# A fused sliding-window attention and MLP kernel: sums apart from products in the opening, four hidden tiles over four banks, stores on another queue

## The chip, the cores and the metric

The kernel runs on one core of a Trainium2 chip. A core has five engines that run side by side, each with its own queue of instructions in order: TensorE (PE in the profile, with its weight loads as PEld), VectorE (DVE), ScalarE (ACT), GpSimd (POOL) and SyncE (SP, which here only issues DMAs). They work on SBUF, TensorE writes its results to PSUM (eight banks), and DMAs move data between the outer memory and SBUF. The metric is the time of one execution on the device, in microseconds (us).

## The reference

Eight batches, eight heads, 576 tokens, head size 64, all inputs in float32. Attention is limited to a window of 32 tokens on either side; its output, with the heads side by side, goes through an MLP of 512 to 2048 to 512 with a leaky ReLU.

```python
scores = scale * np.matmul(q, k.transpose(0, 1, 3, 2))        # scale = 1/8
mask = np.abs(pos[:, None] - pos[None, :]) <= 32
scores = np.where(mask, scores, -1e9)
attn = np.exp(scores - np.max(scores, axis=-1, keepdims=True))
attn = attn / (np.sum(attn, axis=-1, keepdims=True) + 1e-09)
x = np.matmul(attn, v).transpose(0, 2, 1, 3).reshape(4608, 512)
h = x @ w_in                                                   # 512 x 2048
out = np.maximum(0.01 * h, h) @ w_out                          # 2048 x 512
```

## The kernel before

The attention of one batch is cut into eight steps, numbered through all batches: step `i` belongs to batch `i // 8`, half `(i // 4) % 2` of the tokens (288 each) and head pair `i % 4`. Two heads are handled as one: their keys and values stand on the diagonal of 128 x 128 blocks (`kbd`, `vbd`), the rest of which is zero and is cleared once.

What one step does:

- `score(i)`, lines 237 to 253: five matmuls into the PSUM tile `ps` (one buffer of two banks), the exponential `e` on ScalarE, and the product with the window's mask, `pr`, on GpSimd.
- `weighted(i)`, lines 268 to 294: the sums of the probabilities `s` (matmul with a block of ones) and the weighted values `x` (five matmuls with `vbd`), one PSUM bank each; then on VectorE the reciprocal `r` of the sums and the product of `x` and `r`, which lands in `xT`. From step 12 on, `join` first adds the two parts of `pr` on VectorE, so that the sums need one matmul in place of two.

Ahead of them stand, for each pair, the cast of `q` and `k` to bf16 (`cast_qk`), their transposes (on TensorE for batches 0 to 2, with ScalarE copying them out as `qT` and `kT`; by DMA from batch 3 on), `place_keys` (two copies on VectorE into `kbd`), and the cast of the values into `vbd` (`cast_v`, on GpSimd, or in the opening on ScalarE).

The MLP works on halves of 288 tokens: `h_tile(g, f)` (lines 300 to 311) takes four matmuls, one for each head pair, for one of 16 blocks of the hidden width, and an activation on ScalarE into `gT`. `o_tile(j)` (lines 313 to 328) takes 16 matmuls for 128 tokens, a copy `o_sb` on ScalarE and a store that ScalarE issues itself. `h` tiles, output tiles and TensorE's transposes share four PSUM banks (`mmps`).

The order of the work is the order of the program; nothing is rescheduled. The opening (lines 420 to 488) is written out by hand. It loads batch 0 on SP (lines 89 to 96), runs steps 0 to 3 with two or three matmuls without use between them (`keep_busy`), issues the weights' DMAs from GpSimd in between, then loads the keys of batch 1, runs the 16 `h` tiles of half 0 with steps 4 to 7 among them, and the 16 of half 1 with the transposes of batch 1 and scores 8 and 9. The loads of batch 1 are held back by a tiny DMA that reads a weight: the `q` and `k` loads behind the second part of `w_in` (line 459), the `v` loads behind the second part of `w_out` (line 473).

From line 493 on a plan of quarter output tiles and `h` tiles with estimated durations decides when the next step is due; `spend` runs the due steps before each item. In a step of batches 1 to 6 the casts, DMA transposes and loads of later batches are issued too, the DMAs all from SP.

Of the kernel before, what the change touches and what calls it, by code (L numbers as in the profile page):

```python
# [16 lines left out]
def kernel(  # L17
# [31 lines left out]
    cast = ctx.enter_context(tc.tile_pool(name="cast", bufs=1))  # L49
    attn = ctx.enter_context(tc.tile_pool(name="attn", bufs=2))  # L50
    kt = ctx.enter_context(tc.tile_pool(name="kt", bufs=4))
    prob = ctx.enter_context(tc.tile_pool(name="prob", bufs=4))
    tdma = ctx.enter_context(tc.tile_pool(name="tdma", bufs=1))
    outp = ctx.enter_context(tc.tile_pool(name="outp", bufs=4))
    PS = bass.MemoryType.PSUM
# [62 lines left out]
    def clear(t, p):  # L118
        flat = t[:, p].rearrange("p n j -> p (n j)")
        nc.scalar.activation(  # L120
            out=flat, in_=zero.to_broadcast([128, NB * 128]), func=AF.Copy,
        )

    nc.vector.memset(kbd[0], 0.0)
    clear(vbd[0], 0)
    clear(vbd[0], 1)

# [8 lines left out]
    for lo in (0, 64):  # L138
        w = win[lo:lo + 64]
        nc.gpsimd.affine_select(  # L140
            out=w, in_=w, compare_op=ALU.is_ge, fill=0.0,
            base=0, channel_multiplier=-1, pattern=[[0, 3], [1, 128]],
        )
        nc.gpsimd.affine_select(
            out=w, in_=w, compare_op=ALU.is_ge, fill=0.0,
            base=2 * W, channel_multiplier=1, pattern=[[0, 3], [-1, 128]],
        )
    win_f = win.rearrange("p n c -> p (n c)")
    mask = [const.tile([128, NCOL], BF16, name=f"mask{i}") for i in range(2)]

# [86 lines left out]
    def score(i):  # L237
        b, hf, p = where(i)
        ps = scps.tile([128, 1024], FP32, name="ps")
        c0 = 512 - HALF  # L240
        for blk, q0, n in WIN[hf]:
            nc.tensor.matmul(  # L242
                ps[:, c0:c0 + n], kbd[b % 2][:, p, blk],
                qT[b][:, p, q0:q0 + n], start=True, stop=True,
            )
            c0 += n
        e = attn.tile([128, NCOL], BF16, name="e")
        nc.scalar.activation(  # L248
            out=e, in_=ps[:, 512 - HALF:512 - HALF + NCOL], func=AF.Exp, scale=scale,
        )  # L250
        pr = prob.tile([128, NCOL], BF16, name="pr")
        nc.gpsimd.tensor_mul(pr, e, mask[hf])  # L252
        probs[i] = pr, None

    def join(i):


        hf = where(i)[1]
        pr = probs[i][0]
        both = prob.tile([128, HALF], BF16, name="both")  # L260
        o0 = ODD[hf]
        o1 = o0 + NCOL - HALF
        nc.vector.tensor_add(both[:, o0:o1], pr[:, o0:o1], pr[:, HALF:NCOL])  # L263
        rest = slice(0, o0) if o0 else slice(o1, HALF)
        nc.vector.tensor_copy(out=both[:, rest], in_=pr[:, rest])  # L265
        probs[i] = pr, both

    def weighted(i):
        b, hf, p = where(i)
        pr, both = probs.pop(i)  # L270
        x = xps.tile([128, HALF], FP32, name="x")
        s = xps.tile([128, HALF], FP32, name="s")
        if both is not None:
            nc.tensor.matmul(s, ones_bd, both, start=True, stop=True)  # L274
        else:
            nc.tensor.matmul(
                s, ones_bd, pr[:, 0:HALF], start=True, stop=False, skip_group_check=True,
            )
            nc.tensor.matmul(
                s[:, ODD[hf]:ODD[hf] + NCOL - HALF], ones_bd, pr[:, HALF:NCOL],  # L280
                start=False, stop=True, skip_group_check=True,
            )
        c0 = 0
        for n_, (blk, q0, n) in enumerate(WIN[hf]):
            a = q0 - HALF * hf
            nc.tensor.matmul(  # L286
                x[:, a:a + n], vbd[b % 2][:, p, blk, :], pr[:, c0:c0 + n],
                start=(n_ == 0), stop=(n_ == len(WIN[hf]) - 1), skip_group_check=True,
            )
            c0 += n  # L290
        r = attn.tile([128, HALF], FP32, name="r")
        nc.vector.reciprocal(r, s)  # L292
        t0 = (b * S + hf * HALF) % RING
        nc.vector.tensor_mul(xT[:, p, t0:t0 + HALF], x, r)  # L294

    gT = const.tile([128, FFC, RING], BF16)

    def h_tile(g, f):  # L300

        t0 = g * HALF % RING
        h = mmps.tile([128, 512], FP32, name="mm", tag="mm")
        for c in range(DMC):
            nc.tensor.matmul(  # L305
                h[:, 0:HALF], w_in_bf[:, c, ts(f, 128)], xT[:, c, ds(t0, HALF)],
                start=(c == 0), stop=(c == DMC - 1),
            )
        nc.scalar.activation(  # L309
            out=gT[:, f, ds(t0, HALF)], in_=h[:, 0:HALF], func=AF.Prelu, alpha=0.01,  # L310
        )

    def o_tile(j, hook=None):


        cols = (0, 512) if j < NTOK // 128 - 1 else (0, 384, 512)
        for lo, hi in zip(cols[:-1], cols[1:]):
            o = mmps.tile([128, 512], FP32, name="mm", tag="mm")
            for f in range(FFC):
                if hook and lo == 0 and f % 4 == 0:  # L320
                    hook()
                nc.tensor.matmul(  # L322
                    o[:, lo:hi], gT[:, f, ds(128 * j % RING, 128)], w_out_bf[:, f, lo:hi],
                    start=(f == 0), stop=(f == FFC - 1),
                )
            o_sb = outp.tile([128, DMODEL], FP32, name="o_sb")
            nc.scalar.activation(out=o_sb[:, lo:hi], in_=o[:, lo:hi], func=AF.Copy)  # L327
            nc.scalar.dma_start(out=out[ts(j, 128), lo:hi], in_=o_sb[:, lo:hi])

    def keep_busy(n):  # L330


        t = mmps.tile([128, 512], FP32, name="mm", tag="mm")
        for _ in range(n):
            nc.tensor.matmul(t, ones_bd, mask[0][:, 0:512], start=True, stop=True)


    NC = 2 * NPAIR * B
# [22 lines left out]
    def step():  # L361
# [7 lines left out]
        if b > 0:  # L369
            upto = 8 * (b + 1) + (PLAN[b > 1][0][r] if b + 1 < BY_DMA else 0)  # L370
            step_transposes(max(upto - 1, 8 * (b + 1)))
        if i < 7:
            score(i + 1)
        elif 8 <= i < NC - 2:
            nb, _, np_ = where(i + 2)
            if nb >= BY_DMA:
                step_transposes(8 * nb + 2 * np_ + 2)
                place_keys()
            score(i + 2)
# [42 lines left out]
    def first_pair():  # L422
        next(first)
        next(first)
        place_keys()
# [3 lines left out]
    cast_qk(0, 1, nc.vector)  # L429
    first_pair()  # L430
    first_pair()
    clear(vbd[0], 2)
    cast_v(0, 0)
    cast_qk(0, 2, nc.vector)
    score(0)
    load_w_in(0, 512)
    first_pair()
    clear(vbd[0], 3)
    cast_qk(0, 3, nc.vector)
    load_w_in(512, 1024)  # L440
    for i in range(NPAIR):
        score(i + 1)
        if i + 1 < NPAIR:
            cast_v(0, i + 1, on_act=True)
        if i < 2:
            load_w_in(1024 + 512 * i, 1536 + 512 * i)
        else:
            load_w_out(i - 2)
        if i > 0:
            keep_busy(3 if i == 1 else 2)  # L450
        weighted(i)
        if i == 0:
            first_pair()
    state["done"] = NPAIR

    for p in range(NPAIR):
        load_qk(1, p, w_in_bf[0:1, 0, 512:514] if p == 0 else None)
    keep_busy(2)  # L460
    step()
    load_w_out(2)
    load_w_out(3)
    for f in range(FFC):
        h_tile(0, f)
        if f in (2, 6, 10):
            step()
        if f % 4 == 3:
            nc.gpsimd.memset(kbd[1][:, f // 4], 0.0)
    cast_qk(1, 0, nc.vector)  # L470
    cast_qk(1, 1, nc.vector)
    for p in range(NPAIR):
        load_v(1, p, w_out_bf[0:1, 4, 0:2] if p == 0 else None)
    second = transposes(1)
    for f in range(FFC):
        h_tile(1, f)
        if f % 4 == 3:
            p = f // 4
            next(second)
            next(second)  # L480
            place_keys()
            if p + 2 < NPAIR:
                cast_qk(1, p + 2, nc.vector)
            nc.gpsimd.memset(vbd[1][:, p], 0.0)
        if f == 11:
            score(8)
    state["tp"] = 16
    score(9)

# [23 lines left out]
    def spend(us):  # L515
        nonlocal clock, turn
        while due and due[0] <= clock:
            due.pop(0)
            i = state["done"]
            if i < 11:  # L520
                cast_v(1, i - 7)

            if i < 12:
                load_qk(2, i - 8)
            step()
            if 10 <= i < 14:
                load_v(2, i - 10)

        b, p = state["tp"] // 8, state["tp"] % 8 // 2
        turn += 1  # L530
        if kind == "o" and turn % 2 and b >= BY_DMA and (b, p, "k") in qkT and state["done"] > asked[b, p] + 2:
            step_transposes(state["tp"] + 1)
            place_keys()
        clock += us
# [35 lines left out]
```

## Time and profile before

| | |
|---|---|
| six runs, median (lowest to highest) | 328.87 us (327.52 to 331.87) |
| profiled execution, time | 328.19 us |
| profiled execution, span from first to last instruction | 326.5 us |
| TensorE busy, share of the span | 93% |
| first `h` matmul of half 0 starts | 27.6 us |
| first output tile starts | 48.3 us |
| first `h` tile of half 2 starts | 70.0 us |
| reciprocal, 128 x 288 (64 of them), mean | 1954 ns on VectorE |
| product with the mask, 128 x 544 (64), mean | 1218 ns on GpSimd |
| exponential, 128 x 544 (64), mean | 624 ns on ScalarE |
| store of an output tile, from issue to landing, median | 2.1 us |

The profile is of one execution. "Busy" counts instructions of an engine; a matmul's end is modelled, so that matmuls in a row overlap in the records: four `h` matmuls of 286 ns each follow one another in 0.49 us. A row of the timeline has the start in us, the duration, the engine, the line of the program, the operation, and in brackets how long the engine was idle before it and what ended that wait. ACTq and SPq are the DMA issues of ScalarE and SP.

### The profile page before, as it was taken

Reading aid. Unit: us, or ns where it says so; the run is one execution under the profiler, and the core shown is the slowest. Engines: PE = TensorE matmul, PEld = TensorE weight load, DVE = VectorE, ACT = ScalarE, POOL = GpSimd, SP = SyncE. Lnnn points to the kernel's source line nnn. Section 1 sums busy time; section 2 is a strip of 40 time slices with the busy share of each in tenths; the row PEclk is TensorE's granted clock in tenths of the full one; section 3 lists DMA queues with packets and bytes.
Section 4 is the critical chain, followed back from the end, with each engine's and each line's share of the span. In section 5 each row is a group of like instructions: output and inputs, shape, how many; then the busy total and the mean of one; then the engine's idle time right before and its main releaser. Section 6 shows DMA issues by size and latency. Waiting matters only on the chain.

```text
span 326.5 us, 6571 instructions
## 1 busy us (share of the span) xinstructions
PE 304.9 (93%) x2463; PEld 205.1 (63%) x2485; DVE 226.1 (69%) x310; ACT 223.6 (68%) x432; POOL 180.3 (55%) x213
## 2 busy tenths in 40 slices
PE   2578999789999999999999999999999999999996
PEld 1446784457585666767575766667675767676653
DVE  5489744587784988779777988688859867565200
ACT  5774792348395898878787888888786746465441
POOL 7798748657784696429741597249642545131000
PEclk9999999999999999999999999999999999999999
DMA  8999989958999999945994299916831001010102
GB/s 184 221 195 218 269 200 209 251 140 207 218 180 222 200 209 254 196 127 124 214 225 121 75 178 249 207 67 99 191 68 65 34 22 45 0 66 0 67 13 83
DMA packets 85172, 48.28 MB, mean 148 GB/s; under 512 B 64020, under 2 KB 80660, under 8 KB 85140
## 3 DMA queue, kind: packets, MB, share of 16 engines
q1 hardware_dynamic: 75524, 34.22, 54.7%
q10 hardware_dynamic: 5328, 9.44, 8.5%
q0 software_dynamic: 4288, 4.20, 7.8%
q8 instruction: 19, 0.31, 0.4%
q14 instruction: 13, 0.11, 0.1%
HBM read 36.70 MB, written 9.44 MB: 141 GB/s over the span
## 4 chain that ended last, share of the span: by engine, by line
PE 82%; DMA 6%; DVE 5%; SPq 3%; ACT 2%; POOL 1%; issue 1%; ACTq 0%; DVEq 0%
PE mm L305 37%; PE mm L322 33%; PE x L286 4%; PE ps L242 4%; DVE r L292 4%; DMA kf<-in_k_dram 2%; DMA out_dram<-o_sb 2%; PE s L274 2%; DMA vf<-in_v_dram 2%; SPq L83 1%; PE tp L201 1%; SPq L72 1%; DVE xT L294 1%; ACT kT L215 0%; POOL vbd L178 0%
## 5 line engine op out<-in xcount | busy, mean ns | idle before, releaser
L292 DVE RECIPROCAL r<-s 128x288 f32<-128x288 f32 x64 | 125.1, 1954 | 34.4 <-PE s L274 26.0
L252 POOL TENSOR_TENSOR pr<-e,mask 128x544 bf16<-128x544 bf16 x64 | 77.9, 1218 | 102.1 <-ACT e L248 82.2
L305 PE MATMUL mm<-xT,w_in_bf 128*128 128x288 bf16 x1024 | 133.1, 286 | 0.0
L322 PE MATMUL mm<-w_out_bf,gT 128*128 128x512 bf16 (+2 forms) x571 | 128.3, 373 | 1.1
L309 ACT ACTIVATE gT<-mm 128x288 bf16<-128x288 f32 x256 | 101.3, 414 | 22.1 <-PE mm L305 9.4
L305 PEld LDWEIGHTS <-w_in_bf 128*128 128x128 bf16 x1024 | 98.3, 98 | 23.9
L322 PEld LDWEIGHTS <-gT 128*128 128x128 bf16 x592 | 56.5, 98 | 59.8
L248 ACT ACTIVATE e<-ps 128x544 bf16<-128x544 f32 x64 | 40.0, 624 | 25.2 <-ACT o_sb L327 5.7
L327 ACT ACTIVATE o_sb<-mm 128x512 f32<-128x512 f32 (+2 forms) x37 | 21.6, 585 | 45.8 <-PE mm L322 45.8
L227 DVE COPY kbd<-kT 64x576 bf16<-64x576 bf16 x64 | 28.6, 447 | 28.6 <-ACT kT L215 27.9
L178 POOL CAST vbd<-vf 64x576 bf16<-64x576 f32 x58 | 38.7, 668 | 2.1 <-DMA vf<-in_v_dram 0.2
L294 DVE TENSOR_TENSOR xT<-x,r 128x288 bf16<-128x288 f32 x64 | 29.3, 458 | 6.7
L168 POOL CAST kb<-kf 96x768 bf16<-96x768 f32 x32 | 27.3, 854 | 9.3 <-DMA kf<-in_k_dram 9.3
L242 PE MATMUL ps<-qT,kbd 128*128 128x128 bf16 (+2 forms) x320 | 26.6, 216 | 2.2 <-ACT e L248 2.2
L286 PE MATMUL x<-pr,vbd 128*128 128x128 bf16 (+2 forms) x320 | 26.3, 214 | 1.6 <-DVE xT L294 1.3
L242 PEld LDWEIGHTS <-kbd 128*128 128x128 bf16 x320 | 20.8, 101 | 10.5 <-issue 2.6
L263 DVE TENSOR_TENSOR both<-pr 128x256 bf16<-128x256 bf16 x52 | 23.6, 455 | 3.5 <-POOL pr L252 2.5
L286 PEld LDWEIGHTS <-vbd 128*128 128x128 bf16 x320 | 20.8, 99 | 6.4 <-DVE xT L294 2.1
L209 ACT ACTIVATE qT<-qT 128x576 bf16<-128x576 bf16 x20 | 23.6, 1178 | 1.2 <-ACT o_sb L327 1.2
L215 ACT ACTIVATE kT<-kT 128x576 bf16<-128x576 bf16 x20 | 23.5, 1176 | 0.0
L265 DVE COPY both<-pr 128x32 bf16<-128x32 bf16 x52 | 21.1, 405 | 0.0
L168 POOL CAST qb<-qf 96x768 bf16<-96x768 f32 x24 | 19.7, 821 | 0.0
(39 smaller groups left out, 109.8 us busy)
## 6 DMA issues: line engine op xcount, KB each, us to landing
qf<-in_q_dram SPq DMA_DIRECT2D x32, 288.0 KB, 4.9
kf<-in_k_dram SPq DMA_DIRECT2D x32, 288.0 KB, 5.4
vf<-in_v_dram SPq DMA_DIRECT2D x64, 144.0 KB, 5.1
out_dram<-o_sb ACTq DMA_DIRECT2D x35, 256.0 KB, 2.1
w_in_bf<-in_moe_w_in_dram POOLq DMA_DIRECT2D x8, 256.0 KB, 6.7
w_out_bf<-in_moe_w_out_dram POOLq DMA_DIRECT2D x4, 512.0 KB, 14.1
qT<-qb SPq DMA_TRANSPOSE x20, 5.1
kT<-kb SPq DMA_TRANSPOSE x20, 4.0
```

The costliest lines, as they stand in the source:

```text
L168: eng.tensor_copy(out=dst[:, p], in_=src[b, p].rearrange("p a (c d) -> p c a d", d=D),)
L178: nc.gpsimd.tensor_copy(out=vbd[b % 2][r, p, :, r], in_=vf[b, p][r])
L227: nc.vector.tensor_copy(out=kbd[b % 2][r, p, :, r], in_=kT[r].rearrange("p (n j) -> p n j", j=64),)
L242: nc.tensor.matmul(ps[:, c0:c0 + n], kbd[b % 2][:, p, blk], qT[b][:, p, q0:q0 + n], start=True, stop=True,)
L248: nc.scalar.activation(out=e, in_=ps[:, 512 - HALF:512 - HALF + NCOL], func=AF.Exp, scale=scale,)
L252: nc.gpsimd.tensor_mul(pr, e, mask[hf])
L286: nc.tensor.matmul(x[:, a:a + n], vbd[b % 2][:, p, blk, :], pr[:, c0:c0 + n], start=(n_ == 0), stop=(n_ == len(WIN[hf]) - 1), skip_group_c ...
L292: nc.vector.reciprocal(r, s)
L294: nc.vector.tensor_mul(xT[:, p, t0:t0 + HALF], x, r)
L305: nc.tensor.matmul(h[:, 0:HALF], w_in_bf[:, c, ts(f, 128)], xT[:, c, ds(t0, HALF)], start=(c == 0), stop=(c == DMC - 1),)
L309: nc.scalar.activation(out=gT[:, f, ds(t0, HALF)], in_=h[:, 0:HALF], func=AF.Prelu, alpha=0.01,)
L322: nc.tensor.matmul(o[:, lo:hi], gT[:, f, ds(128 * j % RING, 128)], w_out_bf[:, f, lo:hi], start=(f == 0), stop=(f == FFC - 1),)
```

## The change

The opening is written anew; from the first output tile on only the place of a few items differs, and the queue of the stores.

1. `weighted` is split into `sums` (matmuls of the sums and the reciprocal), `product` (matmuls of the values) and `scaled` (the product on VectorE). In steps 0 to 7 the sums of the next step go ahead of later work: sums `i + 1` are issued right after step `i` is scaled.
2. `h_first` computes the first four `h` tiles of halves 0 and 1 together in four PSUM banks, head pair by head pair. In half 0, hooks stand ahead of pair 2 and of pair 3: they run matmuls without use (5, then 8 and 8, of 224 columns, into the free columns of the first bank), the product of step 2 or 3, later sums and scores.
3. Output stores are issued by SP.
4. The `v` loads of batch 1 come right behind its `q` and `k` loads, without the gate.
5. Two of the four clears of `vbd` move: the third to the start of ScalarE's work, the fourth to GpSimd. The clears of `kbd` and `vbd` for batch 1 move within the `h` tiles. The transposes of batch 1's pairs move from behind tiles 3, 7, 11 and 15 of half 1 to behind 5, 9 and 15, the last one into the first output tile, as does score 9.
6. Buffers: `pr` from four to six; `both` from four to two, `r` from two to three, each in a pool of its own.

```diff
-    prob = ctx.enter_context(tc.tile_pool(name="prob", bufs=4))
+    prob = ctx.enter_context(tc.tile_pool(name="prob", bufs=6))
+    joined = ctx.enter_context(tc.tile_pool(name="joined", bufs=2))
+    recip = ctx.enter_context(tc.tile_pool(name="recip", bufs=3))
...
     clear(vbd[0], 1)
+    clear(vbd[0], 2)
...
+    nc.gpsimd.memset(vbd[0][:, 3], 0.0)
...
+    def sums(i):
...
+        r = recip.tile([128, HALF], FP32, name="r")
+        nc.vector.reciprocal(r, s)
+        probs[i][2] = r
+
+    def product(i):
...
+    def scaled(i):
+        _, x, r = probs.pop(i)
+        nc.vector.tensor_mul(place(i), x, r)
+
+    def weighted(i):
+        if probs[i][2] is None:
+            sums(i)
+        product(i)
+        scaled(i)
...
+    def h_first(g, hooks):
+
+        hs = [mmps.tile([128, 512], FP32, name="mm", tag="mm") for _ in range(4)]
         for c in range(DMC):
...
+            if c in hooks:
+                hooks[c](hs[0])
+            for f in range(4):
+                h_mms(g, f, hs[f], (c,))
+        for f in range(4):
+            h_out(g, f, hs[f])
...
-            nc.scalar.dma_start(out=out[ts(j, 128), lo:hi], in_=o_sb[:, lo:hi])
+            nc.sync.dma_start(out=out[ts(j, 128), lo:hi], in_=o_sb[:, lo:hi])
...
-        if i < 7:
-            score(i + 1)
-        elif 8 <= i < NC - 2:
+        if 8 <= i < NC - 2:
...
-    clear(vbd[0], 2)
     cast_v(0, 0)
+    score(0)
     cast_qk(0, 2, nc.vector)
-    score(0)
+    score(1)
     load_w_in(0, 512)
-    first_pair()
-    clear(vbd[0], 3)
+    next(first)
+    sums(0)
+    next(first)
+    product(0)
+    place_keys()
     cast_qk(0, 3, nc.vector)
+    scaled(0)
+    sums(1)
+    cast_v(0, 1, on_act=True)
     load_w_in(512, 1024)
...
+    score(2)
+    load_w_in(1024, 1536)
+    next(first)
+    next(first)
+    place_keys()
+    product(1)
+    scaled(1)
+    cast_v(0, 2, on_act=True)
+    load_w_in(1536, 2048)
+    sums(2)
+    score(3)
+    load_w_out(0)
+    load_w_out(1)
+
+    def before_2(h):
+        keep_busy(h, 5)
+        product(2)
+        scaled(2)
+        cast_v(0, 3, on_act=True)
+        sums(3)
+        score(4)
+        load_w_out(2)
+
+    def before_3(h):
+        keep_busy(h, 8)
+        product(3)
+        scaled(3)
+        sums(4)
+        score(5)
+        load_w_out(3)
+        keep_busy(h, 8)
...
+    def second_half():
+
+        i = state["done"]
+        weighted(i)
+        if i < 7:
+            sums(i + 1)
+        if i < 6:
+            score(i + 2)
+        state["done"] += 1
...
-    keep_busy(2)
-    step()
-    load_w_out(2)
-    load_w_out(3)
-    for f in range(FFC):
+    for p in range(NPAIR):
+        load_v(1, p)
+    h_first(0, {2: before_2, 3: before_3})
+    second_half()
+    for f in range(4, FFC):
         h_tile(0, f)
-        if f in (2, 6, 10):
-            step()
-        if f % 4 == 3:
-            nc.gpsimd.memset(kbd[1][:, f // 4], 0.0)
+        if f in (7, 11):
+            second_half()
+        if f % 2 == 1:
+            nc.gpsimd.memset((kbd if f < 12 else vbd)[1][:, (f - 4) // 2 % 4], 0.0)
...
+    second_half()
     cast_qk(1, 0, nc.vector)
     cast_qk(1, 1, nc.vector)
-    for p in range(NPAIR):
-        load_v(1, p, w_out_bf[0:1, 4, 0:2] if p == 0 else None)
...
+    h_first(1, {})
+    for f in range(4, FFC):
         h_tile(1, f)
...
+        if f in (5, 9, 15):
+            second_pair((f - 5) // 4)
...
+        if f == 13:
             score(8)
     state["tp"] = 16
-    score(9)
...
+        if turn == 2:
+            score(9)
+        if turn == 4:
+            second_pair(3)
```

## The prediction

> **What bounds the kernel now.** I read first the stretches of the span, cut where the order of the work changes: up to the first feed-forward matmul (27.56 us), to the end of the first half's `h` tiles (37.96), to the first output tile (48.34), to the first `h` tile of half 2 (70.0), and the rest. Columns are length, busy us and count of PE, PEld, DVE, ACT, POOL, granted clock, DMA share, GB/s.
>
> ```profile
> PE 304.9 (93%) x2463; PEld 205.1 (63%) x2485; DVE 226.1 (69%) x310; ACT 223.6 (68%) x432; POOL 180.3 (55%) x213
> ...
> 0.00:27.56 27.56, 14.13 (x121) 9.28 (x123) 18.01 (x27) 18.09 (x25) 22.81 (x37) 1.00 1.11 201
> 27.56:37.96 10.40, 10.13 (x100) 8.01 (x97) 9.55 (x9) 7.07 (x17) 8.89 (x10) 1.00 1.19 248
> 37.96:48.34 10.38, 10.38 (x125) 8.79 (x123) 4.93 (x10) 9.85 (x26) 4.51 (x6) 1.00 0.92 218
> 48.34:70.00 21.66, 17.98 (x125) 9.41 (x125) 12.14 (x15) 6.96 (x12) 14.55 (x18) 1.00 1.00 223
> 70.00:322.62 252.62, 251.39 (x1997) 168.93 (x2012) 181.42 (x252) 180.81 (x352) 129.56 (x146) 1.00 0.63 130
> ```
>
> The kernel is bound by PE from 70.0 on: no stall is left there to remove. What can be won lies in the first 27.6 us, where PE works half the time, and in 48 to 70, where 3.7 us are idle (the busy sums include modelled ends of matmuls). So I took the chain of waits of the opening, then the order of time of 52 to 62.
>
> ```profile
> 8.65 7.25 DMA kf<-in_k_dram
> ...
> 19.89 1.97 DVE r L292
> ...
> 21.95 0.46 DVE xT L294
> ...
> 22.41 1.91 DVE r L292
> ...
> 24.41 0.46 DVE xT L294
> ...
> 24.87 1.91 DVE r L292
> ...
> 26.87 0.46 DVE xT L294
> ```
>
> The loads of the fourth pair end at 15.9; from 19.9 on VectorE goes from reciprocal to product without a break, 2.46 us a pair, and `h` begins when the fourth pair (product at 26.87) is placed.
>
> ```profile
> 51.99 0.60 ACT L327 ACTIVATE o_sb<-mm 128x512 f32<-128x512 f32 x1 [2.09 <-PE mm L322]
> ...
> 53.52 0.40 PE L242 MATMUL ps<-qT,kbd 128*128 128x96 bf16 x5
> ...
> 56.02 0.38 ACTq L328 DMA_DIRECT2D out_dram<-o_sb  x1
> ...
> 56.50 0.62 ACT L248 ACTIVATE e<-ps 128x544 bf16<-128x544 f32 x1 [3.91 <-PE mm L322]
> ...
> 57.17 0.40 PE L242 MATMUL ps<-qT,kbd 128*128 128x96 bf16 x5
> ...
> 60.82 0.34 ACTq L328 DMA_DIRECT2D out_dram<-o_sb  x1
> 61.26 0.62 ACT L248 ACTIVATE e<-ps 128x544 bf16<-128x544 f32 x1 [3.64 <-DMA kf<-in_k_dram]
> 61.93 0.40 PE L242 MATMUL ps<-qT,kbd 128*128 128x64 bf16 x5 [2.16 <-ACT e L248]
> ```
>
> The copy `o_sb` is done at 52.59, but its store is issued at 56.02; the next copy ends at 57.61, its store goes at 60.82. ScalarE stands 3.4 and 3.2 us in front of a DMA instruction, and the exponentials behind it (scores finished at 53.9 and 57.6) start at 56.50 and 61.26. Each issue of a store waits on a semaphore of its own and, by the compiled instruction list, on one of eight DMA semaphores that all DMAs of SP and ACT take in turn: the load eight places earlier must have landed. The chain names it: a load of `v` from 50.97 to 55.94, then the store.
>
> **The change part by part.** I walked each engine's new order with durations of the trace.
>
> *Stores from SP (the largest term).* Content of 48.34 to 70.0 at the rates of the PE-bound part: 4 output tiles of 3.45 us (16 matmuls) 13.8, 5 scores of 0.24, 4 sums plus products of 0.48, one joined of 0.37: 17.3 us. 21.66 − 17.3 = 4.4 us are stall, and it follows from the two late exponentials: 2.16 at 61.93, then, as `pr` and `join` come late too, 0.78 before the sums at 69.18, 0.3 before products. With the store on SP the exponentials follow their scores at once. What is late next: VectorE, at 2.42 us a step plus a join of 0.4 to 1.5, against PE's step of about 2.5 (two quarter tiles 1.73, attention 0.75); and GpSimd, which starts the first new probabilities behind the cast of the last `k` (landed at 46.7), then alternates 1.2 of `pr` with 1.4 of `v` casts: I get `v` ready 0.7 to 1.5 us before each product. I leave 0.5 us. Gain 3.9, bounds 2.0 and 4.4.
> On SP each store takes 0.35 us of issue, waits for its copy, and everything behind it waits: loads of batch 2, then DMA transposes. The first pair of batch 3 is the tightest: issued at 93.97 and 95.38, about 4 us to landing, copied at 103.10; two stores now stand ahead of it among eight `v` loads: 0.8 us against 3 us of slack. Later pairs have 5 to 15 us. A store can go out 7 us late behind loads (as at 124.18, before loads issued at 129.36); four `o_sb` buffers allow more than 20, the time to the fourth tile after. Cost nothing.
> Here a rule speaks against the change: the Trainium skill, "DMA: Bandwidth & Descriptors", "Issuing engines are not separate DMA queues", says that the issuing engine changes only the sequencer's time to start a DMA, as all go through the same 16 engines. By the rule the term is 37 × 0.34 us of ScalarE's time off the critical path, so nothing, and the sum would be 327.4. The row shows 3.4 and 3.2 us of waiting in front of the issue, which the rule leaves out; I go by the row.
>
> *Opening.* The clears of `vbd` move from 10.16 and 14.19 to ScalarE's idle time before 5.85 (3 × 1.15 from 2.3, so 5.7) and to GpSimd's idle 4.1 to 5.4 (1.05, as the memset of that shape at line 469). First exponential 10.3 (11.21 before), `pr` 0 at 10.9 (12.86), `pr` 1 after the `k` cast at 12.9 (17.95), first `w_in` chunk issued at 14.1 (14.01; at the median of 6.7 us to landing it is there at about 20.8). Sums first: reciprocal 0 at 13.2 (15.74), but the keys of pair 2 and the `q` cast of pair 3 then stand behind it: 16.7 (15.82). So the fourth pair's transposes end at 18.1 (17.5), its keys are placed at 20.1, its scores start there (19.99 before). VectorE: product 0 17.2, reciprocal 1 17.2 to 19.15, keys 20.1, product 1 20.5, reciprocal 2 to 22.5: that stage is no more than 1 us ahead at this point. GpSimd issues four `w_in` DMAs (0.62 each) ahead of `pr` 3: 21.8 to 23.0.
> PE now has 8 `h` matmuls, 5 fillers and the products of pair 2 in a row from 20.7. At what clock? The rows: products took 0.66 us for five at 19.64 and 0.40 at 22.46, fillers 1.06 for two at 18.16 and 0.59 at 20.46, while the granted clock stands at 1.00. PE reached full rate near 20.2, after a stretch from 16.8 filled by three fillers. The change takes these away. The Trainium skill, "TensorE: Matmul & The Clock Gate", Part 1, says that full rate comes after a busy window of about 3.4 us and Part 4 that transposes do not count as busy. If the row's moment (20.2) held, `h` takes 8 × 0.12, product 2 is placed by 23.0, reciprocal 4 ends at 28.35. By the rule, 12 transposes and two gaps lie in 16 to 20, so full rate comes near 23.6: 8 × 0.24 + 5 × 0.19 + 0.45, product 2 placed at 24.65, reciprocal 3 to 26.6, `pr` 4 26.4, the last four of the 16 `h` matmuls at about 27.7, reciprocal 4 to 29.1, and sums 5 wait for it until then. Then 12 `h` tiles (5.9 us) and four rounds of sums, products and scores: half 1 starts at about 36.2 by the one, 36.95 by the other, 37.96 before. Gain 1.75 or 1.0; I go by the rule, 1.0, bounds 0 and 1.8. The filler of 8 ahead of the last four (0.76) is covered by reciprocal 4; without that cover it is cost.
>
> *By pair over four banks.* Same matmul count (64 a half). When all four banks end together, tile 4 needs the first activation (0.41 + 0.29 after its last matmul, 0.49 given): 0.2 us, once, in half 1; in half 0 attention covers it. Cost 0.2, bounds 0 and 0.6.
>
> *Values of batch 1 behind its keys.* Eight DMAs move ahead of the gate at 38.77; they queue behind `k` (last landed 46.7) and were issued from 45.59 before. Gain 0 to 1 us for data that is cast from 49.8 on; with pair 3's transposes and score 9 moved behind the first output matmuls (0.75 us of the same work): 0. New pools, reciprocals and memsets on GpSimd: same work, buffers at least as deep as are live (two of `both`, three of `r`, three of six `pr`): 0. The tail: ACT issued at 323.14 between copies that waited for PE anyway: 0.
>
> Sum: 1.0 − 0.2 + 3.9 = 4.7. The profiled execution took 328.19 (span 326.5), so 323.5. It stands 0.7 below the median of the six (328.87), so I expect **324.0** in a median.
>
> **Rivals.**
> *Opening gives nothing (0.12).* If PE stays at half rate into 26 us, pair 3 is placed at 28 or later, and the 12 `h` matmuls done early (1.47 us) only pay that back: 325.2. For: VectorE's chain hardly moves. Against: PE is dense from 19.3 on.
> *The loads bound 48 to 70 (0.08).* `k` lands at 46.7 and the batch 2 loads now follow stores; if casts and `pr` set the steps, half of the stall stays (gain 2.0): 326.1. For: DMA share 1.00 there. Against: the waits name ScalarE's exponentials, not casts.
> *SP becomes the bound: slower (0.08).* Place: SP, one queue in order, 171 rows become 207, with stores waiting for PE ahead of transposes (1.2 us of issue each, two a pair). A transposed pair is asked ten steps before use for most pairs; if SP falls more than 10 us behind, ScalarE waits in front of the copy of `qT`, and every batch from 3 to 7 loses; 2.5 us each are 12.5, less 4.7: 336.7. It decides for slower above 1.6 us a batch (8 us in all). For: SP issues nearly without break from 94 to 137. Against: later it waits up to 15 us for casts, so it is ahead.
> *The change does what it says* is not in doubt for the stores; that scores follow earlier is the forecast (0.72).
>
> **How the numbers follow.** The likeliest case, 324.0, has bounds from its terms of 321.8 (gains of 1.8 and 4.4, less 0.2, and 0.4 for the values, off 328.19) to 327.1 (gains of 0 and 2.0, less 0.2, off the median), which take in the two rivals on the near side: 321.8 to 327.2. Left out are the slow rival and a little at each end. One per cent of 328.87 is what a measurement of this kernel tells from no change: below 325.6 is faster, above 332.2 slower. Faster: most of the main case (0.63) and half of the opening rival (0.06), 0.69; slower: 0.09; the rest, 0.22, within.
>
> **What would show it.** Right: stores in SP's rows, exponentials of steps 10 and 11 within 0.1 us of their scores, no wait of PE for `e` between 47 and 65, first `h` tile of half 2 near 65.3, the first `h` matmul near 20.7 and half 1 at 37. Products of pair 2 at 0.66 or 0.40 tell the clock. Wrong: ScalarE waiting for a DMA at `o_sb`, or at `qT`/`kT` after 100 us; PE idle over 1 us in 48 to 65; fewer than 252 us busy after half 2 begins, with waits.

## The result, and the profile after

The changed kernel takes 327.2 us in the median, against 328.6 of the kernel before run beside it on the same chips: ratio 0.9957, interval 0.9942 to 0.9973. So it is faster by 0.4%, where 1.4% was forecast. One of its 19 executions took 703 us, for a reason that the record does not show, and is not in the ratio. The profiled executions stand at 327.01 (span 325.3) and 328.19 (span 326.5); the 1.2 us between the spans can be followed stage by stage.

The stretches of the span after, cut at the same events as in the prediction (first `h` matmul, end of the 16 `h` tiles of half 0, first output tile, first `h` tile of half 2); only the ends of the last rows, 322.62 and 322.00, are not at the same event. The columns are those of the prediction's first table:

```profile
0.00:21.81 21.81, 9.91 (x84) 6.57 (x85) 14.97 (x23) 14.55 (x20) 19.35 (x33) 1.00 1.10 198
21.81:38.10 16.29, 15.31 (x145) 12.56 (x146) 12.76 (x11) 9.59 (x23) 12.68 (x14) 1.00 1.20 230
38.10:48.60 10.50, 10.01 (x110) 8.05 (x107) 6.10 (x10) 8.66 (x23) 7.07 (x8) 1.00 1.22 243
48.60:66.97 18.37, 18.06 (x142) 10.27 (x143) 11.95 (x17) 7.61 (x14) 13.99 (x16) 1.00 0.93 203
66.97:322.00 255.03, 252.37 (x2009) 169.53 (x2023) 180.83 (x252) 183.00 (x355) 129.38 (x146) 1.00 0.65 132
```

The `h` matmuls start 5.8 us earlier, yet half 1 starts at 38.10 (before: 37.96). The first output tile starts at 48.60 (48.34), although 0.75 us of transposes and a score were moved behind it. Half 2 starts at 66.97 (70.0). And in the last stretch, where no loss was expected, TensorE idles 2.7 us (1.2 before). The starts of the groups of `h` tiles (16 tiles, one half of the tokens) show where: from the fifth group to the seventh the time is 34.91 us before (109.99 to 144.90) and 36.68 after (106.96 to 143.64); all later groups keep their distance. The sum of what was gained, stage by stage: −0.14 (opening) − 0.12 (half 1) + 3.29 (output tiles) − 1.77 (the two groups) = 1.26.

All four come from one pair of executions. For the first two, runs below have the same instructions, so that more profiles can be set beside them. Half 1 starts at 37.96, 38.91 and 39.04 in the three profiles with the old opening (before, e1, e9), and at 38.10, 38.43, 39.39 and 38.78 in the four with the new one (after, e2, e3, e4): both scatter by over 1 us, around 38.6 and 38.7. So the new opening is worth nothing that these profiles can show. From the start of half 1 to the first output tile it takes 10.37 to 10.38 us in the three, and 10.09, 10.09, 10.09 and, in the changed kernel's profile alone, 10.50 in the four.

**The opening.** The chain of waits after, up to half 1 (start, duration, what):

```profile
13.54 1.17 POOL pr L256
14.72 0.75 POOL w_in_bf L454
15.46 6.21 DMA w_in_bf<-in_moe_w_in_dram
21.68 0.14 issue
21.81 2.08 PE mm L328 x8
23.89 0.92 PE mm L376 x5
24.82 0.24 PE x L299 x5
...
28.32 0.63 ACT e L252
28.95 0.08 issue
29.03 1.21 POOL pr L256
30.24 0.04 issue
30.29 0.28 PE s L280
```

Up to half 1 the chain no longer names VectorE. It names a load of the first `w_in` chunk, the second of its two DMAs, then eight `h` matmuls at half rate (2.08 us; eight take 0.98 later on), then five matmuls without use, all of which stand in TensorE's order ahead of product 2 (`x`). From 25 us on rounds of sums, scores, exponential and mask product follow. VectorE had been idle for 2.25 us when product 2 came; its timeline:

```profile
25.09 0.46 DVE L314 TENSOR_TENSOR xT<-x,r 128x288 bf16<-128x288 f32 x1 [2.25 <-PE x L299]
```

**The output tiles.** ScalarE's timeline and SyncE's, around the first two stores:

```profile
53.01 0.60 ACT L369 ACTIVATE o_sb<-mm 128x512 f32<-128x512 f32 x1
55.03 0.62 ACT L252 ACTIVATE e<-ps 128x544 bf16<-128x544 f32 x1 [1.43 <-PE ps L246]
```

```profile
53.63 0.38 SPq L370 DMA_DIRECT2D out_dram<-o_sb  x1
```

The exponential now waits for its scores alone, and the store leaves as soon as its copy is there. The stretch takes 18.37 us with 0.75 us more work in it than the 21.66 before: 4.0 us of stall are gone.

**The new wait, at 121 to 131.** VectorE's timeline after:

```profile
121.59 0.29 DVE L267 TENSOR_TENSOR both<-pr 128x256 bf16<-128x256 bf16 x1
121.80 1.20 DVE L269 COPY both<-pr 128x32 bf16<-128x32 bf16 x1
122.92 1.95 DVE L288 RECIPROCAL r<-s 128x288 f32<-128x288 f32 x1
...
126.27 0.81 DVE L267 TENSOR_TENSOR both<-pr 128x256 bf16<-128x256 bf16 x1
127.00 0.79 DVE L269 COPY both<-pr 128x32 bf16<-128x32 bf16 x1
```

GpSimd's after, and TensorE's:

```profile
121.76 1.21 POOL L256 TENSOR_TENSOR pr<-e,mask 128x544 bf16<-128x544 bf16 x1 [1.47 <-issue]
...
126.11 0.82 POOL L172 CAST qb<-qf 96x768 bf16<-96x768 f32 x1
...
126.88 0.89 POOL L172 CAST kb<-kf 96x768 bf16<-96x768 f32 x1
```

```profile
124.92 0.28 PE L278 MATMUL s<-both,ones_bd 128*128 128x288 bf16 x1 [1.00 <-DVE r L288]
125.48 0.41 PE L299 MATMUL x<-pr,vbd 128*128 128x96 bf16 x5 [0.28 <-DVE xT L314]
```

And VectorE's copy of the same step before, with GpSimd's product:

```profile
124.85 0.17 DVE L265 COPY both<-pr 128x32 bf16<-128x32 bf16 x1
```

```profile
125.38 1.22 POOL L252 TENSOR_TENSOR pr<-e,mask 128x544 bf16<-128x544 bf16 x1 [1.46 <-issue]
```

A copy of 32 columns that takes 0.17 us took 1.20: it ends at 123.00, GpSimd's product with the mask at 122.97. In the kernel before that product starts at 125.38, after the join. The exponential ahead of that product now follows the output copy at once (121.00), where it stood idle for 0.47 us around the store's issue before; so GpSimd's product falls on the join, the reciprocal behind it in VectorE's order starts 1 us late, and TensorE waits for it. In the next step the join meets GpSimd's casts of `q` and `k` (126.11 and 126.88), and its two parts take 0.81 and 0.79. This agrees with what the Trainium skill says in "SBUF — State Buffer", "Who interferes with whom": the two engines share a pair of ports, held for a whole instruction by one of them, and a copy of VectorE can be an instruction that needs it.

Such meetings are not new. The page's row for that copy, before and after:

```profile
L265 DVE COPY both<-pr 128x32 bf16<-128x32 bf16 x52 | 21.1, 405 | 0.0
```

```profile
L269 DVE COPY both<-pr 128x32 bf16<-128x32 bf16 x52 | 22.7, 437 | 0.0
```

The mean of 52 was 405 ns before and is 437 ns now, against 0.17 us for one alone. What is new is that one of them stands where TensorE waits behind it.

### The profile page after: what moved, and what is told of

It is laid out like the page before. It is cut to its first block, busy times and chain, and to the rows that moved or that the text cites. A ratio compares the mean times of both kernels' runs of the same rounds, so it can differ in the third digit from the quotient of the medians.

```text
span 325.3 us, 6617 instructions
## 1 busy us (share of the span) xinstructions
PE 305.9 (94%) x2476; PEld 207.0 (64%) x2497; DVE 226.6 (70%) x310; ACT 223.7 (69%) x431; POOL 182.5 (56%) x214
## 4 chain that ended last, share of the span: by engine, by line
PE 81%; POOL 6%; DMA 4%; DVE 4%; ACT 3%; issue 1%; SPq 0%; ACTq 0%; POOLq 0%; DVEq 0%
PE mm L364 35%; PE mm L328 34%; PE ps L246 4%; PE x L299 4%; DMA w_in_bf<-in_moe_w_in_dram 2%; POOL pr L256 2%; DMA kf<-in_k_dram 2%; PE s L278 2%; DVE r L288 2%; PE tp L205 1%; POOL kb L172 1%; ACT e L252 1%; POOL kbd L545 1%; ACT kT L219 1%; POOL vbd L545 1%
## 5 line engine op out<-in xcount | busy, mean ns | idle before, releaser
L288 DVE RECIPROCAL r<-s 128x288 f32<-128x288 f32 x64 | 125.1, 1955 | 38.7 <-PE s L278 35.4
L328 PE MATMUL mm<-xT,w_in_bf 128*128 128x288 bf16 x1024 | 134.8, 287 | 0.8 <-DMA w_in_bf<-in_moe_w_in_dram 0.6
L334 ACT ACTIVATE gT<-mm 128x288 bf16<-128x288 f32 x256 | 103.8, 411 | 23.7 <-PE mm L328 8.5
L172 POOL CAST kb<-kf 96x768 bf16<-96x768 f32 x32 | 28.4, 890 | 4.0 <-DMA kf<-in_k_dram 3.9
L246 PEld LDWEIGHTS <-kbd 128*128 128x128 bf16 x320 | 20.7, 100 | 11.0 <-DVE kbd L231 2.8
L213 ACT ACTIVATE qT<-qT 128x576 bf16<-128x576 bf16 x20 | 23.6, 1180 | 0.0
L269 DVE COPY both<-pr 128x32 bf16<-128x32 bf16 x52 | 22.7, 437 | 0.0
L267 DVE TENSOR_TENSOR both<-pr 128x256 bf16<-128x256 bf16 x52 | 21.0, 404 | 0.6
```

What stands on the lines that cost most here:

```text
L172: eng.tensor_copy(out=dst[:, p], in_=src[b, p].rearrange("p a (c d) -> p c a d", d=D),)
L246: nc.tensor.matmul(ps[:, c0:c0 + n], kbd[b % 2][:, p, blk], qT[b][:, p, q0:q0 + n], start=True, stop=True,)
L328: nc.tensor.matmul(h[:, 0:HALF], w_in_bf[:, c, ts(f, 128)], xT[:, c, ds(g * HALF % RING, HALF)], start=(c == 0), stop=(c == DMC - 1),)
L334: nc.scalar.activation(out=gT[:, f, ds(g * HALF % RING, HALF)], in_=h[:, 0:HALF], func=AF.Prelu, alpha=0.01,)
```

## The experiments

All ratios are to the kernel before, run beside the experiment on one chip, with 95% intervals. e1 to e4 take the change apart, e5 to e12 look for what holds the opening.

### e1: the stores alone

```diff
 (the kernel before)
-            nc.scalar.dma_start(out=out[ts(j, 128), lo:hi], in_=o_sb[:, lo:hi])
+            nc.sync.dma_start(out=out[ts(j, 128), lo:hi], in_=o_sb[:, lo:hi])
```

> The kernel before with one edit: output stores issued by SP. Theory: the store term was sized right (4.0 us between the first output tile and the first h tile of half 2) and the new opening adds nothing or loses about 1 us; so this kernel alone has that stretch near 17.5 us in place of 21.66, the exponentials of scores 10 and 11 within 0.1 us of their scores, and a time near 325 (326.5 if the stretch from 121 to 131 us loses 1.8 us here too, since exponentials and so GpSimd's products come about 0.5 us earlier against VectorE's joins). Rival: the stall in that stretch is set by the loads of batch 1 and goes only with the earlier values; then this kernel stays at 328 or above and PE still waits over 1.5 us there.

327.34 us, ratio 0.9958 (0.9941 to 0.9975): one line of the change gives all of its gain. From the first output tile to half 2 it is 17.90 us (21.66 before). The loss is there as well: 36.67 us from the fifth to the seventh group of `h` tiles, with the same wait in TensorE's timeline:

```profile
125.14 0.28 PE L274 MATMUL s<-both,ones_bd 128*128 128x288 bf16 x1 [1.02 <-DVE r L292]
```

So the collision belongs to the stores' move, not to the new opening. The time lies above the 326.5 that was expected with this loss. The first output tile starts at 49.28 here and at 48.34 in the kernel before, and up to that point the two programs are the same: one profile places the opening only to about 1 us. That is 0.9 of the 1.5 us by which the two profiled spans (326.5 and 326.0) fall short of what the stages give (3.76 − 1.77); the rest stands behind the last `h` tiles.

### e2: all but the stores

```diff
 (the changed kernel)
-            nc.sync.dma_start(out=out[ts(j, 128), lo:hi], in_=o_sb[:, lo:hi])
+            nc.scalar.dma_start(out=out[ts(j, 128), lo:hi], in_=o_sb[:, lo:hi])
```

> The changed kernel with one edit undone: output stores issued by ScalarE again. Theory: the stall between the first output tile and half 2 comes back (about 3.5 to 4 us, ScalarE in front of a store), the opening's small loss stays, and the 1.8 us lost between 110 and 131 us go because ScalarE is held 0.4 us by each store again: 329 to 330. Rival (the gain is due to the opening and the early values): stays near 327.2.

330.24 us, ratio 1.005 (1.0034 to 1.0065): the rest of the change, without the stores, makes the kernel slower. ScalarE's timeline, then TensorE's:

```profile
52.93 0.60 ACT L369 ACTIVATE o_sb<-mm 128x512 f32<-128x512 f32 x1
57.30 0.38 ACTq L370 DMA_DIRECT2D out_dram<-o_sb  x1
57.79 0.62 ACT L252 ACTIVATE e<-ps 128x544 bf16<-128x544 f32 x1 [4.26 <-DMA kf<-in_k_dram]
```

```profile
63.66 0.40 PE L246 MATMUL ps<-qT,kbd 128*128 128x64 bf16 x5 [2.60 <-ACT e L252]
```

The copy ends at 53.53 and the store is issued at 57.30, 0.07 us after the landing (57.23) of the load issued eight DMAs earlier; the wait in front of it grew from 3.4 to 3.8 us. The stretch to half 2 is 23.20 us, 4.8 more than in the changed kernel. From the fifth to the seventh group it is 34.91 again, to the hundredth the time before.

### e3: one store back on ScalarE

```diff
-            nc.sync.dma_start(out=out[ts(j, 128), lo:hi], in_=o_sb[:, lo:hi])
+            (nc.scalar if j == 9 else nc.sync).dma_start(out=out[ts(j, 128), lo:hi], in_=o_sb[:, lo:hi])
```

> The changed kernel, but the store of output tile 9 alone is issued by ScalarE. Theory (collision): this holds the next exponential by 0.4 to 0.5 us, the mask product on GpSimd starts after VectorE's small join copy in place of beside it, that copy takes 0.17 us in place of 1.20, the reciprocal after it starts about 0.9 us earlier and the wait of PE for it (1.0 us at 124) nearly goes: 0.5 to 1 us off the time, 326.3 to 326.7. Rival (SP: the transposed keys come late behind the stores): one store moved changes nothing, PE still waits 1.0 us there, 327.2.

326.58 us, ratio 0.9927 (0.9901 to 0.9953). Tile 9 is the one whose copy stands ahead of the exponential at 121. VectorE's timeline, then GpSimd's:

```profile
122.69 0.17 DVE L269 COPY both<-pr 128x32 bf16<-128x32 bf16 x1
...
126.46 1.20 DVE L269 COPY both<-pr 128x32 bf16<-128x32 bf16 x1
```

```profile
126.41 1.21 POOL L256 TENSOR_TENSOR pr<-e,mask 128x544 bf16<-128x544 bf16 x1 [0.60 <-POOL vbd L182]
```

The issue in front of the exponential (0.38 us) shifts GpSimd's product off the first copy, which is at 0.17 again. The second step's copy now meets its own product, starts with it and ends with it. The time of the two groups is 35.67: half of the loss is gone.

### e4: no joins where they collide

```diff
-        if JOINED - 1 <= i < NC - 1:
+        if JOINED - 1 <= i < NC - 1 and i + 1 not in (24, 25):
```

> The changed kernel, but steps 24 and 25 are not joined on VectorE: their sums take two matmuls on PE in place of one (0.11 us more each). Theory: VectorE is late in that stretch because the joins stand ahead of the reciprocals and collide with GpSimd; without the two joins PE's waits of 1.0, 0.28, 0.3 and 0.28 us go and the stretch from the first h tile of half 4 to the second output tile after it is 1.5 us shorter: about 325.6. Rival (SP, late transposed keys): the copies of the keys stay late, less than 0.5 us gained, 326.8 or more.

325.67 us, ratio 0.9903 (0.9874 to 0.9932). The sums of steps 24 and 25 take two matmuls in place of a join and one. The two groups take 34.73 us, the timeline lists no wait of TensorE between 105 and 150, and the reciprocal follows `place_keys` at once. Together with e3, which keeps the joins and shifts one of them out of the meeting, that shows the joins slowed by GpSimd ahead of the reciprocal as the cause of the 1.77 us. e5 to e8 and e10 to e12 are built on e4.

### e5: the weights asked for first

```diff
     cast_qk(0, 2, nc.vector)
+    load_w_in(0, 512)
     score(1)
-    load_w_in(0, 512)
```

> The kernel without joins 24 and 25, and the first two w_in DMAs issued by GpSimd ahead of the mask product of step 1 in place of behind it. Theory: in the new opening everything from 21.8 us on hangs on the landing of that chunk (PE waited 0.6 to 1.3 us for it, with xT of pairs 0 and 1 ready at 21.0), so issue about 1.2 us earlier makes the first h matmul start near 21 and takes 0.6 to 1.0 us off the time: 324.7 to 325.1. Rival (the DMA rate sets the landing, not the issue): the chunk lands when it did, 325.7, and later by the delay of the mask product if anything.

325.55 us, ratio 0.9896 (0.9873 to 0.9918): e4's. The first issue moved to 14.06 (14.53 in e4), TensorE's wait stayed:

```profile
22.77 2.08 PE L328 MATMUL mm<-xT,w_in_bf 128*128 128x288 bf16 x8 [0.58 <-DMA w_in_bf<-in_moe_w_in_dram]
```

The chunk comes in two DMAs, and the `h` matmuls need both. The second landed at 21.59 (before), 21.68 (after), 22.05 (e4) and, though issued 0.48 us earlier than in e4, 22.64 (e5). Batch 0 is still landing then, and the share of the DMA engines stands at 1.10 in this stretch of the changed kernel. An earlier issue did not bring the weights earlier here; what sets their landing was not tried.

### e6: scores one step further ahead

```diff
+    def before_1(h):
+        score(4)
...
-        score(4)
+        score(5)
...
-        if i < 6:
-            score(i + 2)
+        if i < 5:
+            score(i + 3)
```

> The kernel without joins 24 and 25, and scores 4 to 7 issued one step earlier (score 4 between the h matmuls of pair 0 and those of pair 1). Theory: the chain of sums, scores, exponential and mask product (2.7 us a round from 26 to 33) is broken, PE no longer waits for GpSimd's products before sums 4 and 5, and VectorE (2.46 us a pair) sets the pace again: half 1 starts 0.3 to 0.8 us earlier, 325.0 to 325.4. Rival (only VectorE's late start of product 2, at 25.1, matters): 325.7 or worse by the 0.4 us that score 4 takes ahead of product 2.

325.1 us, ratio 0.9887 (0.9865 to 0.9908). TensorE's waits for `pr` are gone (one for `r`, 0.45 us, in their place), but half 1 starts at 39.06, no earlier than e4's 38.78: VectorE now stands idle for 3.41 us until product 2. What the rounds of scores give is taken by the later start. The time lies where it was forecast, but half 1 does not, and the interval overlaps that of e4: no success of the theory.

### e7: no filler ahead of product 2

```diff
     def before_2(h):
-        keep_busy(h, 5)
         product(2)
```

> The kernel without joins 24 and 25, and without the five matmuls without use ahead of product 2. Theory: they stand in the chain at 23.9 to 24.8; without them product 2 comes 0.9 us earlier, and both VectorE and the scores behind it too: 324.9 or so. Rival (clock): they are what brings PE to full rate at 24.9, without them products 2 and 3, sums and scores run at half rate for longer (0.66 us in place of 0.44 for five) and half of the gain or all of it goes: 325.3 to 325.8.

324.71 us, ratio 0.9881 (0.9857 to 0.9905). Product 2 starts 1.88 us behind the first `h` matmul (2.81 in the changed kernel) and takes 0.66 us in place of 0.44; half 1 follows 15.72 us behind the first `h` matmul (16.59 in e4). The fillers cost 0.9 us on the path, and the rate that they warmed up gave back 0.2 on the product. In the time, 0.96 us below e4's, the intervals overlap.

### e8: e5, e6 and e7 together, and four clears moved

```diff
+        if f in (5, 6, 7, 9):
+            nc.gpsimd.memset(vbd[1][:, (5, 6, 7, 9).index(f)], 0.0)
```

> The three edits together, and the clears of batch 1's values moved behind the cast of its first keys on GpSimd. Theory: the first h matmul near 21, product 2 near 23, VectorE without a gap from there, half 1 at 36.5 in place of 38.1 to 38.8 and the first output tile near 47: 323.3 to 324.0. Rival (loads): the first output tile cannot move much since k of batch 1 lands at 46 to 47, 325.

325.23 us, ratio 0.9892 (0.9866 to 0.9918). All clears of `vbd` for batch 1 now stand behind its first `k` cast on GpSimd. The first output tile starts at 47.82, the earliest of all, but half 2 only at 67.64: 19.82 us, where e4 takes 18.36. VectorE's timeline, then GpSimd's and TensorE's:

```profile
47.08 3.07 DVE L172 CAST qb<-qf 96x768 bf16<-96x768 f32 x1 [0.77 <-DMA qf<-in_q_dram]
...
63.72 1.18 DVE L269 COPY both<-pr 128x32 bf16<-128x32 bf16 x1
```

```profile
46.18 3.05 POOL L566 MEMSET vbd<- 128x1152 bf16 x3
49.18 1.65 POOL L172 CAST kb<-kf 96x768 bf16<-96x768 f32 x1
...
63.63 1.24 POOL L256 TENSOR_TENSOR pr<-e,mask 128x544 bf16<-128x544 bf16 x1 [0.15 <-ACT e L252]
```

```profile
66.82 0.28 PE L278 MATMUL s<-both,ones_bd 128*128 128x288 bf16 x1 [0.66 <-DVE r L288]
```

A cast of 0.56 us took 3.07 among GpSimd's clears, but no wait of TensorE follows it. What TensorE waits for is the reciprocal behind a join: its copy took 1.18 us beside the product with the mask. It is the collision again, at another join, and it costs what was won. The time is neither the 323.3 to 324.0 of the theory nor told apart from e4's.

### e9: the old opening with the two good edits

```diff
 (the kernel before)
-            nc.scalar.dma_start(out=out[ts(j, 128), lo:hi], in_=o_sb[:, lo:hi])
+            nc.sync.dma_start(out=out[ts(j, 128), lo:hi], in_=o_sb[:, lo:hi])
-        if JOINED - 1 <= i < NC - 1:
+        if JOINED - 1 <= i < NC - 1 and i + 1 not in (24, 25):
```

> The kernel before with two edits alone: output stores issued from SyncE, and steps 24 and 25 summed by products instead of joins. The new opening, the four score banks and the moved values are left out. Theory (the new opening and half 1 are worth nothing in sum): 325.4 to 326.0 us, the time of the changed kernel without joins 24 and 25 (325.67), stretch of steps 4 and 5 of the half 1 loop near 34.8. Rival (they are worth 1 us, which something else hides): 326.5 or more.

325.54 us, ratio 0.9922 (0.9891 to 0.9952), beside e4's 325.67: the new opening, the four banks and the moved values are together worth nothing that can be measured, within intervals of about 0.3% (1 us) to either side. Half 2 starts at 67.19 here and at 67.23 in e4.

### e10: product 2 ahead of the wait for the weights

```diff
-    def before_2(h):
-        keep_busy(h, 5)
+    def before_0(h):
         product(2)
         scaled(2)
         cast_v(0, 3, on_act=True)
+
+    def before_1(h):
         sums(3)
...
-    h_first(0, {2: before_2, 3: before_3})
+    h_first(0, {0: before_0, 1: before_1, 2: before_2})
```

> The changed kernel without joins 24 and 25, without the five filler products, and with product 2 of the opening ahead of the first h matmuls in TensorE's order. Theory (TensorE in order behind its wait for w_in is what held product 2 back and idled VectorE for 2.25 us): product 2 about 1 us ahead of the first h matmul instead of 1.9 behind it, first output-side phase of half 1 at 36.0 to 37.0, time 323.0 to 324.2 us. Rival (GpSimd's mask products, or the landing of loads, set the pace of the rounds anyway): half 1 no earlier than 37.8, time 324.6 or more.

The edit also takes out the fillers around product 3 (8 and 8) and moves the work of each hook at least one head pair ahead; the excerpt shows this in part. The same holds for e12.

324.31 us, ratio 0.987 (0.9841 to 0.9899), the lowest of the study, but its interval overlaps that of e7. TensorE's timeline:

```profile
21.73 0.66 PE L299 MATMUL x<-pr,vbd 128*128 128x96 bf16 x5
23.65 1.12 PE L328 MATMUL mm<-xT,w_in_bf 128*128 128x288 bf16 x4 [1.26 <-DMA w_in_bf<-in_moe_w_in_dram]
24.56 0.45 PE L280 MATMUL s<-pr,ones_bd 128*128 128x288 bf16 x1
```

Product 2 is 1.9 us ahead of the first `h` matmul, as meant. Half 1 starts at 38.25, not at 36 to 37. The weights came later in this execution, and the sums of tile 3, now behind the wait for them, hold VectorE back for 1.22 us. So the theory falls as to half 1, and the time lies between its range and the rival's: once product 2 is out of the way, the wait only holds the next one.

### e11: the values of batch 1 gated as before

```diff
 (e7)
-    for p in range(NPAIR):
-        load_v(1, p)
     h_first(0, {2: before_2, 3: before_3})
...
+    for p in range(NPAIR):
+        load_v(1, p, w_out_bf[0:1, 4, 0:2] if p == 0 else None)
```

> The changed kernel without joins 24 and 25 and without the filler products, but with the values of batch 1 issued behind the last part of w_out again, as in the kernel before. Theory (that move is worth nothing): 324.7 plus or minus 0.3 us. Rival (early values let half 1 run): 1 us or more slower, with TensorE waits for v in half 1.

325.62 us, ratio 0.9908 (0.9879 to 0.9936), against e7's 0.9881 (0.9857 to 0.9905). The difference of 0.9 us lies outside the theory's 0.3, but the intervals overlap, and no wait for `v` appears in half 1. The two profiled executions differ by 1.8 us, and 1.1 of them are there before the edit can bear: the first `h` matmul starts at 23.45 (22.32). This stays open.

### e12: the mask product of tile 3 ahead of two weight issues

```diff
 (e10)
-    load_w_in(1536, 2048)
     sums(2)
     score(3)
+    load_w_in(1536, 2048)
```

> The previous kernel (no joins 24 and 25, no filler products, product 2 ahead of the h matmuls) with the two issues of the last quarter of w_in moved behind the mask product of tile 3 on GpSimd. Theory (with TensorE's order mended, those 1.2 us of issues ahead of the mask product of tile 3 are what keeps VectorE idle for 1.22 us before that tile's reciprocal): mask product 3 at 22.7 instead of 23.2 us, reciprocal 3 about 0.5 us earlier, first 24-matmul stretch of half 1 at 37.8 instead of 38.25, time 323.8 us. Rival (the h matmuls' wait for w_in, which stands ahead of the sums of tile 3, sets it): reciprocal 3 no earlier against the first h matmul than now (1.6 us behind it), time 324.3 plus or minus 0.3.

324.71 us, ratio 0.9895 (0.9868 to 0.9923), not told apart from e10. The mask product starts at 22.52 (23.22 in e10), but the reciprocal of tile 3 stands 1.61 us behind the first `h` matmul in both (24.55 behind 22.94; 25.26 behind 23.65), and half 1 starts at 38.27. The wait for the weights sets the reciprocal, not GpSimd. Half 1 gains nothing from weights that came 0.71 us earlier either: TensorE's next wait for a mask product grew from 0.78 to 1.38 us.

## Why the prediction was wrong

The forecast was 4.7 us off the profiled execution; 1.2 came. Stage by stage, the loss behind the stores, the opening and the four banks took 1.77, 1.14 and 0.67 more than was put, and the stores gave 0.14 more: 4.7 − 1.77 − 1.14 − 0.67 + 0.14 = 1.26. By its steps:

- **Stores from SP: right.** 3.9 was put, 4.0 measured in the changed kernel, 3.76 in e1 (21.66 − 17.90). The row (3.4 and 3.2 us in front of an issue) was the better guide than the rule that the prediction set against it; e2, which puts that wait back, lost 0.9% against the changed kernel (1.005 / 0.9957). That the wait is for one of eight semaphores taken in turn was not tried apart, but the traces fit: three stores are issued 0.07 to 0.08 us after the DMA eight places earlier has landed (55.94 and 56.02, 60.74 and 60.82, in e2 57.23 and 57.30). The slow rival, SP as the bound, did not come: ScalarE has no idle time before its copies of `qT` and `kT` from DMA (0.0 us in the page).
- **"Cost nothing" behind the stores: this failed, by 1.77 us.** The prediction asked what is late next up to 70 us and said that "no stall is left there to remove" from there on; it did not ask what an earlier exponential would meet there. GpSimd's product behind it met the join of VectorE. Its own figure for a join, "0.4 to 1.5" us, was the sign that a join can be slow. e1 shows that the stores bring the loss, e3 and e4 that taking the meeting, or the join, away removes it.
- **Opening: 1.0 was put, −0.14 came,** just below the lower bound of 0; the seven profiles above put it near 0. The first `h` matmul was put at 20.7 and came at 21.81: the median of 6.7 us to landing was counted from the first of the chunk's two DMAs, and the `h` matmuls need the second as well. Counted from that one (issued at 14.81 in the kernel before) it gives 21.5. So product 2 was placed at 25.55 in place of 24.65. The step on the clock was right: eight `h` matmuls and five fillers took 3.0 us (2.87 put), and product 2 ran at 0.44 from 24.62 on, nearer the rule's moment (23.6) than the row's (20.2). What was also not right was to count half 1's start from reciprocal 4: sums 5 came at 30.29 and not at 29.1, behind GpSimd's mask product (the chain above), a round of scores, exponential and mask of 2.7 us where VectorE's 2.46 had been the pace. In e5, e10 and e12 the order of issues on GpSimd and of products on TensorE shifts half 1 by less than the scatter of 1 us. e9 gives the value of all of it directly: none that can be measured.
- **Four banks: 0.2 was put, 0.87 came** in half 1 (10.50 us with 0.75 less work, 10.38 before). Of this, 0.36 are in this profile and in those of e5 and e7 alone: TensorE's wait for a `k` cast, which stands on GpSimd behind five clears that the change put there (35.6 to 41.0). In e2, e3 and e4, with the same instructions and 10.09 us, the cost is 0.46, inside the bound of 0.6. Some 0.3 of that are the wait for the first of four banks, as the prediction's mechanism has it; the rest was not followed.
- **Values early: 0 was put,** and e11 doesn't contradict it clearly.
- **"Opening gives nothing"** (325.2, chance 0.12) came true in its effect, for another reason than its own: TensorE reached full rate near 24.6 us, not after 26. The rival "loads" lies nearer in number (326.1), but its stall did not come: the stretch to half 2 has 0.3 us idle.

The changed kernel without joins 24 and 25 and without fillers (e7, e10, e12) takes 324.3 to 324.7. That this lies near the forecast of 324.0 is luck: about 3 us come from the stores and the mended collision (e9, 325.54), and the last 1 us, if it is one (the intervals overlap), from the opening without fillers, another opening than the one that was forecast.

## What to carry to other kernels

When a change makes one engine faster, follow the work that it sets free to the next engine, and look there for instructions of a neighbour that it now runs beside; here a copy of 32 columns on VectorE took seven times its time beside GpSimd, and handed its delay to the reciprocal behind it. Such meetings happen all along; the ones that cost are those behind which the bounding engine waits. A DMA issue is an instruction in its engine's order: give it to an engine with nothing urgent behind it. And judge a new opening where its gain has to arrive, in more than one profile: matmuls started 5.8 us earlier here, and at half 1 nothing was left of it.

## What the runs showed of the hardware

- A VectorE copy of 128x32 bf16 took 0.17 us alone and 1.20 beside GpSimd's product with the mask, both in the changed kernel and in e3, each time ending with GpSimd's instruction to 0.05 us. A copy that started 0.04 us ahead of such a product (130.33 and 130.37, changed kernel) took 0.17. A cast of 96x768 took 3.07 in place of 0.56 among GpSimd's clears (e8).
- The first weights landed later in the kernel that asked for them earlier: the second DMA of the first chunk was issued at 14.85 and landed at 22.64 us in e5, 15.33 and 22.05 in e4.
- The start of the first output tile differs by 0.9 us between two executions that have the same instructions up to there (48.34 and 49.28), while the stretches from half 2 on agree to some hundredths.
